# A zero column for the warm-up, K'V turned ahead of K'V, and a 304/208 split of the experts' second layer

## The chip, the core and the metric

The kernel runs on one core of a Trainium2 chip. The core has a matrix engine (TensorE: PE in the rows, with its weight loads as PEld), a vector engine (VectorE, DVE), an activation engine (ScalarE, ACT), GpSimd (POOL) and SyncE (SP), which here issues nearly all DMAs. Each engine runs its own instructions in order and waits on semaphores for the others. The metric is the device time of one execution in microseconds (us).

## The reference, cut to what matters

Three layers follow each other on 2304 tokens (4 batches of 576), all in float32.

```python
# 1. linear attention, 8 heads of 64; phi(x) = [exp(p - max|p|), exp(-(p - max|p|))], p = x @ w_phi (64 -> 128)
kv  = einsum('bhsf,bhsd->bhfd', phi(k), v);  z = phi(k).sum(s)
x   = (phi(q) @ kv) / (phi(q) @ z + 1e-6)                 # -> 2304 x 512
# 2. gated layer with RMS norm
xn  = x / rms(x) * g
x   = (silu(xn @ w_gate) * (xn @ w_val)) @ w_out          # 512 -> 1536 -> 512
# 3. soft mixture: 32 slots = 8 experts x 4
logits = x @ phi                                          # 2304 x 32
slot_input = softmax_over_tokens(logits).T @ x            # 32 x 512
slot_out[e] = relu(slot_input[e] @ w1[e]) @ w2[e]         # 512 -> 1024 -> 512, 8 experts
out = softmax_over_slots(logits) @ slot_out               # 2304 x 512
```

## The kernel before

The program has four stages, one after the other on PE.

**K stage** (0 to 116 us of the span). For each of 18 tiles of 128 tokens, K is projected (`P`, L501), DVE takes the largest magnitude and subtracts it (L505, L509), ACT takes both exponentials (`kp`, L522 and L523), and PE adds the products with V and with ones into three accumulators of the batch (`kacc`, L546 and L555). A batch has 576 tokens, so it ends in the middle of a tile: the loop then does `k.kv(parts[0])` for the old batch, `finish()`, `kn.project()` for the tile after next, and `k.kv(parts[-1])` for the new one. `finish()` makes an `Evac`: three copies of the accumulators to SBUF (`kvs0` to `kvs2`, L568 and L570), and three `turn`s, put into the list `fillers`. A turn is four PE transposes into a PSUM tile of three rotating ones (`misc`, shared with Q's projections `P` of L387) and two copies out of it into `kvt` (L592 on DVE for turn 1, L594 on ACT for turns 0 and 2). The loop pops one filler in each of a tile's two half steps, after `k.kv(parts[-1])`. Between these run the first block of Q (`Rows`: L387, L402, the products `o` of L447, the row scaling `y` of L467, the transposes `yT` of L474) and the conversion of nine weight pieces (`Conv`: L144, L146 on ACT; L154, L156, L122 on DVE, 1.2 us each). The order of instructions within this stage is made by a scheduler from the code, so a moved line moves others too.

At its start PE runs matmuls whose result nobody reads (`warm`, L608: `idle<-still`), four before the first projection and three after the second. `still` is a 128x256 tile that DVE sets to zero.

**Gated layer** (116 to 643 us): six blocks of 384 tokens, 12 strips of 128 hidden columns each. Its code is untouched.

**Router and slots** (643 to 653.6 us): `finish` in `post`; untouched.

**Experts and combination** (653.6 us to the end). 32 loads of 1 MB (`unit(n)`, L694) bring w1 (units 0 to 15) and w2 (16 to 31), in that order, into slots that come free as earlier weights are used. `fc1` multiplies the slot rows with w1 in 18 groups of four matmuls of 512 columns. `fc2(e, r, half)` does w2: `half` is which 512 of the 1024 hidden values, `r` which part of the 512 output columns (`RCOLS`: 256 and 256); a call is one group of four matmuls that run side by side on PE's four column strips. Before, unit 16 + e holds all hidden values of the first 256 columns and unit 24 + e those of the last 256. `slots(r)` copies the sum (DVE, L1118), adds the four strips by a matmul (`so`, L1120) and scales it (DVE, L1121, L1122). `combine(r, blk)` multiplies the weights of 384 tokens with it in nine matmuls (`op`, L1136), copies three tiles out (DVE and ACT in turn, L1140, L1142) and issues the output DMA of the block (L1146; L1144 one by one for block 0). The order of PE within the experts is the order of the code in `experts()` (it is `placed`).

Of the kernel before, what the change touches and what calls it, by code (L numbers as in the profile page):

```python
# [30 lines left out]
CFIRST = 7  # L31
WARM = 4
WARM2 = 3
RCOLS = [256, 256]
CEVERY = 3
PADDED = [3.5, 3.5, 3.5, 6, 6.5, 18.5, 13.5]
PLAST = [2, 2, 2, 6, 9, 15, 12]
# [29 lines left out]
def tile_kernel(ctx: ExitStack, tc: tile.TileContext, q2T, qT, kT, v, wbd, wg, wv, wo, rmsg, phi, w1, w2, consts, out):  # L67
# [409 lines left out]
    with ExitStack() as pk:  # L477
# [121 lines left out]
        ks = [K(sp, psk, kT, i, kb if i else dict(kb, P=("misc", 3))) for i in range(TILES)]  # L599
        ks[0].load(ACT)  # L600
        SP.dma_start(out=wbd_f, in_=wbd)
        still = sp.tile([128, 256], F32, tag="kvs0", name="still", bufs=1)
        DVE.memset(still, 0.0)
        DVE.memset(ones_sb, 1.0)
        idle = psk.tile([32, 256], F32, tag="acc0", name="idle", bufs=1)
        def warm(n, w):
            for _ in range(n):
                PE.matmul(out=idle[:, 0:w], lhsT=still[:, 0:32], rhs=still[:, 0:w], start=True, stop=True)  # L608

        warm(WARM, 256)  # L610
        for r in range(2):
# [23 lines left out]
        for i in range(TILES):  # L635
            k, kn = ks[i], ks[i + 2] if i + 2 < TILES else None
            if i + 4 < TILES:
                ks[i + 4].load()
            if i + 2 < TILES:
                ks[i + 2].load_v()  # L640
            parts = batch_parts(i)
            b = parts[0][0]
            ends = i * 128 + parts[0][2] == (b + 1) * SEQ

            def finish():
                ev = Evac(b)
                fillers.extend([lambda n=n: ev.turn(n) for n in range(3)])

            if len(parts) > 1:
                k.kv(parts[0])  # L650
                finish()
            if kn:
                kn.project()
                kn.shift(0)
                kn.shift(1)
            k.kv(parts[-1])
            for hf in range(2):
                if kn:
                    kn.exps(hf)
                n = 2 * i + hf - CFIRST  # L660
                if (n + 5) % 3 == 0 and 0 <= n + 5 and (n + 5) // 3 < NPRE:
                    placed(lambda: conv_load(sp, KCONV, sp), SP.engine)
                if n >= 0:
                    if n % 3:
                        conv_join()
                    else:
                        conv_parts()
                        conv_scale()
                if fillers:
                    fillers.pop(0)()  # L670
                for f in qsteps[2 * i + hf]:
                    f()
            if ends and len(parts) == 1:
                finish()
# [401 lines left out]
    with ExitStack() as p3:  # L1076
# [28 lines left out]
            ho.fill(lambda o, i: ACT.activation(out=o, in_=i, func=AF.Relu), h, 4 * half, 4 * half + 4)  # L1105

        def fc2(e, r, half):
            u = unit((2 + r) * NE + e).rearrange("p (k d) -> p k d", k=8)
            for c in range(4):
                k = 4 * half + c  # L1110
                PE.matmul(out=y2[r][32 * c:32 * c + 32], lhsT=ho[e, k], rhs=u[:, k],  # L1111
                          start=e == 0 and half == 0, stop=e == NE - 1 and half == 1)

        def slots(r):

# [32 lines left out]
        def experts():  # L1148
# [9 lines left out]
            turn1(1)  # L1158
            for e in range(2, NE):
                fc2(e, 0, 0)  # L1160
            for e in range(NE):
                fc2(e, 0, 1)
            blk = 0
            for e in range(NE):
                fc2(e, 1, 0)
                fc2(e, 1, 1)
                if e == 0:
                    slots(0)
                if e in (2, 5, 7):
                    for blk in range(blk, blk + (2 if e < 7 else 1)):  # L1170
                        combine(0, blk)
                    blk += 1
            slots(1)
            combine(0, blk)
# [7 lines left out]
def _layout(inputs):  # L1182
    import numpy as np

    def heads(a):
# [22 lines left out]
        "rmsg": np.asarray(inputs["moe_rms_g"]).reshape(4, 128).T,  # L1208
        "phi": np.asarray(inputs["moe2_phi"]).reshape(4, 128, NS).transpose(1, 0, 2).reshape(128, 4 * NS),
        "w1": np.asarray(inputs["moe2_w1"]).reshape(NE, 4, 128, 2, 512).transpose(0, 3, 2, 1, 4).reshape(NE, 2, 128, 2048),  # L1210
        "w2": np.asarray(inputs["moe2_w2"]).reshape(NE, 8, 128, 2, 256).transpose(0, 3, 2, 1, 4).reshape(NE, 2, 128, 2048),
        "consts": consts,
    }

# [19 lines left out]
```

## Time and profile before

| | us |
|---|---|
| median of 3 runs (700.24 to 700.74) | 700.58 |
| the profiled execution | 701.1 |
| its span | 699.3 |
| PE busy | 687.5 (98%) |
| DVE, ACT, POOL busy | 469.8, 328.1, 146.6 |
| end of PE's last instruction | 692.0 |

The profiled execution is 1.8 us longer than its span, and 0.5 us longer than the median. In the page's forty slices PE is at 90% or more in all but the first and the last, DVE at 80 to 90% or more in most of the first seven. The output DMAs fill the last 7 us alone.

### The profile page before, as it was taken

How to read it: one execution, taken by the hardware profiler on the slowest of the kernel's cores; microseconds unless marked ns; L12 is line 12 of the kernel's file. 1: busy time of each engine (PE TensorE's matmuls, PEld its weight loads, DVE VectorE, ACT ScalarE, POOL GpSimd, SP SyncE). 2: the span in 40 equal slices, each digit the busy share in tenths (PEclk: the TensorE clock that was granted, in tenths of full speed). 3: DMA queues.
4: the chain of work that ended last, by engine and by line, in shares of the span. 5: the costliest groups of instructions: out<-in, count | busy, mean ns of one | idle time of the engine just before them, and what ended most of it. 6: DMA issues, size and time to landing. Idle time of an engine off the chain costs nothing.

```text
span 699.3 us, 11901 instructions
## 1 busy us (share of the span) xinstructions
PE 687.5 (98%) x4715; PEld 570.8 (82%) x4715; DVE 469.8 (67%) x914; ACT 328.1 (47%) x686; POOL 146.6 (21%) x74
## 2 busy tenths in 40 slices
PE   8999999999999999999999999999999999999995
PEld 5667666988889898998979989899897999898453
DVE  4899995988875695766857669676685753323423
ACT  4878885687745444344432554425444231112202
POOL 0000000000003355133651336422364200000100
PEclk9999999999999999999999999999999999999997
DMA  7755534434210001010000100001000085477977
GB/s 258 256 186 175 193 123 166 144 121 164 78 40 27 7 23 32 0 58 12 24 0 1 57 13 24 0 1 57 1 1 0 1 314 228 180 264 276 372 303 260
DMA packets 24216, 77.66 MB, mean 111 GB/s; under 512 B 2528, under 2 KB 12640, under 8 KB 17760
## 3 DMA queue, kind: packets, MB, share of 16 engines
q1 hardware_dynamic: 24016, 76.64, 30.9%
q8 instruction: 37, 0.61, 0.4%
q10 hardware_dynamic: 144, 0.26, 0.1%
q14 instruction: 19, 0.16, 0.1%
HBM read 71.11 MB, written 5.78 MB: 110 GB/s over the span
## 4 chain that ended last, share of the span: by engine, by line
PE 96%; DMA 1%; ACT 1%; DVE 0%; issue 0%; SPq 0%; DVEq 0%; ACTq 0%
PE pv L952 22%; PE pg L952 22%; PE acc L977 7%; PE acc L978 7%; PE acc L979 7%; PE kacc L546 5%; PE num L221 4%; PE kacc L555 3%; PE P L501 3%; PE y L1111 2%; PE y L1095 2%; PE o L447 2%; PE P L387 1%; PE x2tp L742 1%; PE op L1136 1%; PE qP L313 1%
## 5 line engine op out<-in xcount | busy, mean ns | idle before, releaser
L952 PE MATMUL pv<-xnh,wv 128*128 128x384 f32 x576 | 117.1, 342 | 0.0
L952 PE MATMUL pg<-xnh,wg 128*128 128x384 f32 x576 | 114.7, 341 | 0.3 <-ACT xnh L119 0.3
L316 POOL PARTITION_ALL_REDUCE qe<-qe x32 | 51.9, 1634 | 295.7 <-ACT qe L315 286.5
L952 PEld LDWEIGHTS pg<-xnh,wg 128*128 128x128 f32 x576 | 102.8, 188 | 6.2 <-ACT xnh L119 0.7
L952 PEld LDWEIGHTS pv<-xnh,wv 128*128 128x128 f32 x576 | 101.9, 188 | 4.9 <-DVE qe L346 3.4
L347 POOL PARTITION_ALL_REDUCE qe<-qe x32 | 82.1, 2613 | 85.0 <-DVE qe L346 66.4
L119 ACT CAST hh<-t 128x384 fp32r<-128x384 f32 x72 | 36.6, 509 | 115.8 <-PE acc L978 75.5
L977 PE MATMUL acc<-wo,hh 128*128 128x512 f32 x216 | 87.1, 403 | 0.0
L978 PE MATMUL acc<-wo,hh 128*128 128x512 f32 x216 | 86.1, 398 | 0.0
L979 PE MATMUL acc<-wo,hl 128*128 128x512 f32 x216 | 85.2, 394 | 0.0
L122 DVE TENSOR_TENSOR hl<-t,hh 128x384 fp32r<-128x384 f32 x72 | 40.0, 556 | 65.1 <-ACT hh L119 64.9
L960 DVE SCALAR_TENSOR_TENSOR t<-t,pg 128x384 f32<-128x384 f32 x72 | 39.6, 550 | 57.7 <-ACT t L959 57.5
L959 ACT ACTIVATE t<-pg 128x384 f32<-128x384 f32 x72 | 35.1, 487 | 72.5 <-PE pg L952 72.1
L952 PE MATMUL pg<-xnl,wg 128*128 128x384 f32 x288 | 64.9, 341 | 0.0
L952 PE MATMUL pv<-xnl,wv 128*128 128x384 f32 x288 | 62.4, 338 | 0.0
L964 DVE TENSOR_TENSOR t<-t,pv 128x384 f32<-128x384 f32 x72 | 39.5, 549 | 25.3 <-PE pv L952 24.3
L952 PEld LDWEIGHTS pg<-xnl,wg 128*128 128x128 f32 x288 | 51.9, 188 | 1.5 <-DVE xnl L122 0.9
L952 PEld LDWEIGHTS pv<-xnl,wv 128*128 128x128 f32 x288 | 51.7, 188 | 0.0
L979 PEld LDWEIGHTS acc<-wo,hl 128*128 128x128 f32 x216 | 40.6, 188 | 10.2 <-DVE hl L122 0.3
L977 PEld LDWEIGHTS acc<-wo,hh 128*128 128x128 f32 x216 | 40.8, 189 | 7.4 <-issue 0.3
L978 PEld LDWEIGHTS acc<-wo,hh 128*128 128x128 f32 x216 | 40.6, 188 | 6.4
L546 PE MATMUL kacc<-kp,vt 128*64 128x256 f32 (+1 forms) x320 | 39.8, 386 | 0.0
(206 smaller groups left out, 1047.3 us busy)
## 6 DMA issues: line engine op xcount, KB each, us to landing
eu<-in_w_dram SPq DMA_DIRECT2D x32, 1024.0 KB, 6.4
wraw<-in_wg_dram SPq DMA_DIRECT2D x6, 1024.0 KB, 4.8
wraw<-in_wv_dram SPq DMA_DIRECT2D x6, 1024.0 KB, 5.7
wraw<-in_wo_dram SPq DMA_DIRECT2D x6, 1024.0 KB, 5.1
qraw<-in_qT_dram SPq DMA_DIRECT2D x32, 192.0 KB, 2.3
vt<-in_v_dram SPq DMA_DIRECT2D x18, 256.0 KB, 2.9
raw<-in_kT_dram SPq DMA_DIRECT2D x17, 256.0 KB, 3.2
out_dram<-ob SPq DMA_DIRECT2D x10, 384.0 KB, 3.5
```

The lines of the kernel that those rows point to most:

```text
L119: ACT.copy(out=hi, in_=src)
L122: (lo_eng or POOL).tensor_tensor(out=lo, in0=src, in1=hi.bitcast(F32), op=ALU.subtract)
L316: POOL.partition_all_reduce(e[:, 0], e[:, 1], channels=128, reduce_op=bass_isa.ReduceOp.absmax)
L347: POOL.partition_all_reduce(e[hh][:, 1], u, channels=128, reduce_op=bass_isa.ReduceOp.add)
L546: PE.matmul(out=kva[o0:o0 + 64, hh // 2], lhsT=self.vt[r0:r1, h], rhs=kp[r0:r1, hh].rearrange("p s f -> p (s f)"), start=first and hh < 2, ...
L952: PE.matmul(out=p, lhsT=w[:, a, c], rhs=x, start=n == 0, stop=n == 11)
L959: ACT.activation(out=t, in_=g, func=AF.Tanh, scale=0.5)
L960: DVE.scalar_tensor_tensor(out=t, in0=t, scalar=1.0, in1=g, op0=ALU.add, op1=ALU.mult)
L964: DVE.tensor_tensor(out=t, in0=t, in1=wide("v", m, xs), op=ALU.mult)
L977: PE.matmul(out=acc[i], lhsT=hh[:, s], rhs=w[:, 0], start=m == 0, stop=False)
L978: PE.matmul(out=acc[i], lhsT=hh[:, s], rhs=w[:, 1], start=False, stop=False)
L979: PE.matmul(out=acc[i], lhsT=hl[:, s], rhs=w[:, 0], start=False, stop=m == MF - 1)
```

## The change

- `still` becomes a constant column of zeros that GpSimd sets before the program starts; both operands of the unread products read it with a step of zero. DVE's memset goes.
- In the tile in which batch 1 begins (`b == 0` there), the first filler, turn 0 of batch 0's K'V, is popped before `k.kv(parts[-1])`; turns 1 and 2 each come one half step earlier.
- `RCOLS` becomes 304 and 208. w2 is laid out so that unit 16 + e holds the first 512 hidden values with all 512 columns and unit 24 + e the other 512. Each part r now reads all 16 units. The order in `experts()`: all of r = 0 for the first halves, the second halves of experts 0 to 5, two groups of r = 1 (expert 0), the second halves of experts 6 and 7, then the other 14 groups of r = 1 with `slots(0)` after two of them and one block of `combine(0, .)` after 5, 7, 10, 12 and 14.

```diff
-RCOLS = [256, 256]
+RCOLS = [304, 208]
...
-        still = sp.tile([128, 256], F32, tag="kvs0", name="still", bufs=1)
-        DVE.memset(still, 0.0)
+        still = nc.const_aps.tensor(0.0, [128, 1], F32)
...
-                PE.matmul(out=idle[:, 0:w], lhsT=still[:, 0:32], rhs=still[:, 0:w], start=True, stop=True)
+                PE.matmul(out=idle[:, 0:w], lhsT=still.to_broadcast([128, 32]), rhs=still.to_broadcast([128, w]), start=True, stop=True)
...
                 kn.shift(1)
+            if fillers and b == 0:
+                fillers.pop(0)()
             k.kv(parts[-1])
...
         def fc2(e, r, half):
-            u = unit((2 + r) * NE + e).rearrange("p (k d) -> p k d", k=8)
+            u = unit((2 + half) * NE + e).rearrange("p (k d) -> p k d", k=4)
...
-            for e in range(NE):
+            for e in range(6):
+                fc2(e, 0, 1)
+            second = [(e, half) for e in range(NE) for half in range(2)]
+            for e, half in second[:2]:
+                fc2(e, 1, half)
+            for e in range(6, NE):
                 fc2(e, 0, 1)
             blk = 0
-            for e in range(NE):
-                fc2(e, 1, 0)
-                fc2(e, 1, 1)
-                if e == 0:
+            for n, (e, half) in enumerate(second[2:]):
+                fc2(e, 1, half)
+                if n == 1:
                     slots(0)
-                if e in (2, 5, 7):
-                    for blk in range(blk, blk + (2 if e < 7 else 1)):
-                        combine(0, blk)
+                if n in (4, 6, 9, 11, 13):
+                    combine(0, blk)
                     blk += 1
```

**PE, K stage, where batch 0 ends (29 to 46 us).** `kacc` are products of K' with V or with ones (the numbers are those of batch 1), `kvt` the transposes of a turn. Before:

```order
L546 MATMUL kacc_438<-kp,vt 64x256 x4
L546 MATMUL kacc_439<-kp,vt 64x256 x4
L555 MATMUL kacc_440<-kp,small 32x256 x8
L583 MATMUL kvt<-cst,kvs_413 128x128 x4
L387 MATMUL P<-wbd_f,qraw 128x256
L583 MATMUL kvt<-cst,kvs_415 128x128 x4
L387 MATMUL P<-wbd_f,qraw 128x256
L501 MATMUL P<-wbd_f,raw 128x128 x8
L546 MATMUL kacc_438<-kp,vt 64x256 x4
L546 MATMUL kacc_439<-kp,vt 64x256 x4
L555 MATMUL kacc_440<-kp,small 32x256 x8
L583 MATMUL kvt<-cst,kvs_417 128x128 x4
```

Now:

```order
L583 MATMUL kvt<-cst,kvs_411 128x128 x4
L546 MATMUL kacc_443<-kp,vt 64x256 x4
L546 MATMUL kacc_444<-kp,vt 64x256 x4
L555 MATMUL kacc_445<-kp,small 32x256 x8
L583 MATMUL kvt<-cst,kvs_413 128x128 x4
L387 MATMUL P<-wbd_f,qraw 128x256
L583 MATMUL kvt<-cst,kvs_415 128x128 x4
L501 MATMUL P<-wbd_f,raw 128x128 x3
L387 MATMUL P<-wbd_f,qraw 128x256
L501 MATMUL P<-wbd_f,raw 128x128 x5
L546 MATMUL kacc_443<-kp,vt 64x256 x4
L546 MATMUL kacc_444<-kp,vt 64x256 x4
```

The first turn stands ahead of the sixteen products, the other two follow one place earlier each, and Q's second projection stands behind three of the next tile's eight K projections.

**DVE, end of the K stage (96 to 109 us).** From the scaling of the last product `o` of Q's block 0 towards the row scaling; `wt`, `wv`, `wo` are weight pieces. Before:

```order
L122 TENSOR_TENSOR wv_1310<-wt,wv_1310 128x1024
L154 SCALAR_TENSOR_TENSOR wt<-wt,wraw 128x1024
L450 TENSOR_SCALAR rd<-o 128x6
L592 COPY kvx<-kvt 128x2x2x64
L451 RECIPROCAL rd<-rd 128x6
L592 COPY kvx<-kvt 128x2x2x64
L452 TENSOR_TENSOR y<-o,rd 128x3x128
L505 TENSOR_REDUCE mx<-P 128x4 x2
L509 TENSOR_TENSOR pr<-P,mx 128x512 x2
L464 TENSOR_SCALAR ms<-ms 128x3
L156 SCALAR_TENSOR_TENSOR wt<-wraw,wt 128x1024
L196 TENSOR_SCALAR rs<-ms 128x3
```

Now:

```order
L450 TENSOR_SCALAR rd<-o 128x6
L156 SCALAR_TENSOR_TENSOR wt<-wraw,wt 128x1024
L451 RECIPROCAL rd<-rd 128x6
L592 COPY kvx<-kvt 128x2x2x64
L452 TENSOR_TENSOR y<-o,rd 128x3x128
L592 COPY kvx<-kvt 128x2x2x64
L505 TENSOR_REDUCE mx<-P 128x4 x2
L509 TENSOR_TENSOR pr<-P,mx 128x512 x2
L464 TENSOR_SCALAR ms<-ms 128x3
L122 TENSOR_TENSOR wv_1308<-wt,wv_1308 128x1024
L196 TENSOR_SCALAR rs<-ms 128x3
L122 TENSOR_TENSOR wo_1369<-wt,wo_1369 128x1024
```

Between `L450` and the row scaling (L467, further on in both) stood two operations of 128x1024 (`L156` and, later, `L122` of `wo`); now there are three, since `L122` of `wv` has come from in front of `L450`.

**PE, experts, around the end of the first column part.** `y` with the lower number is part 0, with the higher part 1; `eu` are the loads. Before:

```order
L1111 MATMUL y_6490<-eu_6390,ho 32x256 x4
L1111 MATMUL y_6491<-eu_6653,ho 32x256 x8
L1120 MATMUL so<-y2s,cst 96x256
L1111 MATMUL y_6491<-eu_6669,ho 32x256 x8
L1111 MATMUL y_6491<-eu_6679,ho 32x256 x8
L1136 MATMUL op<-SO_6494,cT 128x256 x18
L1111 MATMUL y_6491<-eu_6724,ho 32x256 x8
L1111 MATMUL y_6491<-eu_6734,ho 32x256 x8
L1111 MATMUL y_6491<-eu_6744,ho 32x256 x8
L1136 MATMUL op<-SO_6494,cT 128x256 x18
```

Now (`eu_6663` and `eu_6669` are units 30 and 31, the last two loads):

```order
L1111 MATMUL y_6488<-eu_6649,ho 32x304 x4
L1111 MATMUL y_6489<-eu_6289,ho 32x208 x4
L1111 MATMUL y_6489<-eu_6619,ho 32x208 x4
L1111 MATMUL y_6488<-eu_6663,ho 32x304 x4
L1111 MATMUL y_6488<-eu_6669,ho 32x304 x4
L1111 MATMUL y_6489<-eu_6291,ho 32x208 x4
L1111 MATMUL y_6489<-eu_6625,ho 32x208 x4
L1120 MATMUL so<-y2s,cst 96x304
L1111 MATMUL y_6489<-eu_6293,ho 32x208 x4
L1111 MATMUL y_6489<-eu_6631,ho 32x208 x4
L1111 MATMUL y_6489<-eu_6335,ho 32x208 x4
L1136 MATMUL op<-SO_6492,cT 128x304 x9
```

Part 0 is complete only after the last load; before, it needed none of the last eight. The blocks of `op` stand one at a time instead of two. SP's order of loads is the same.

## Rows read from the trace of the kernel before

**Rows 1.** The page, part 4: shares of the chain that ended last.

```profile
PE 96%; DMA 1%; ACT 1%; DVE 0%; issue 0%; SPq 0%; DVEq 0%; ACTq 0%
```

**Rows 2.** Timeline, all engines, first 12 us: start, length, engine, line, operation, count.

```profile
0.24 0.10 POOL L1223 MEMSET const-float32-0.0<- 128x1 f32 x1 [0.24 <-issue]
...
0.85 0.27 DVE L603 MEMSET still<- 128x256 f32 x1 [0.85 <-PEq L1223]
1.08 0.09 DVE L604 MEMSET small<- 128x32 f32 x1
...
1.18 3.62 PE L608 MATMUL idle<-still 128*32 128x256 f32 x8 [1.18 <-DVE small L604]
...
4.73 2.42 PEld L501 LDWEIGHTS P<-wbd_f,raw 64*128 64x128 f32 x32 [0.81 <-DMA raw<-in_kT_dram]
...
7.27 1.48 PE L608 MATMUL idle<-still 128*32 128x256 f32 x6
```

**Rows 3.** The chain that ended last, first 46 us: start, length, what.

```profile
36.68 1.06 ACT wraw L146
...
38.77 0.55 ACT kv L594 x2
...
41.16 1.88 PE kacc L546 x16
43.03 1.00 PE kacc L555 x16
44.03 0.59 PE kvt L583 x4
...
44.84 0.43 PE P L387 x2
```

**Rows 4.** Timeline, all engines, 29 to 46 us.

```profile
31.48 0.58 ACT L570 COPY kvs<-kacc 128x512 f32<-128x512 f32 x1
...
35.99 1.21 DVE L154 SCALAR_TENSOR_TENSOR wt<-wt,wraw 128x1024 uint32<-128x1024 uint32 x1
...
39.25 0.41 DVE L592 COPY kv<-kvt 128x256 f32<-128x256 f32 x1
...
39.36 0.70 PE L387 MATMUL P<-wbd_f,qraw 128*128 128x256 f32 x2 [1.47 <-ACT kv L594]
```

**Rows 5.** Timeline, all engines, 96 to 111 us.

```profile
97.98 0.16 DVE L450 TENSOR_SCALAR rd<-o 128x6 f32<-128x6 f32 x1 [0.32 <-PE o L447]
...
108.30 1.27 DVE L467 TENSOR_SCALAR y<-y,ms 128x512 f32<-128x512 f32 x3
...
109.72 0.96 PEld L474 LDWEIGHTS yT<-cst,y 128*128 128x128 f32 x9 [0.41 <-DVE y L467]
```

**Rows 6.** The chain that ended last, 640 us to the end.

```profile
668.27 0.86 PE y L1111 x16
669.13 0.60 PE hp L1102 x4
669.74 7.04 PE y L1111 x128
...
680.16 2.73 PE y L1111 x48
682.89 0.91 PE op L1136 x18
```

**Rows 7.** SP's last load (unit 31) alone: its issue, and the time to its landing.

```profile
L694 SPq DMA_DIRECT2D eu<-in_w_dram x1: 328/328/328, 663.2 to 663.2; - x1
...
DMA to landing us min/median/max: 15.6/15.6/15.6
```

**Rows 8.** SP's output DMA of block 5 of part 0 alone.

```profile
L1146 SPq DMA_DIRECT2D out_dram<-ob x1: 462/462/462, 688.7 to 688.7; - x1
```

**Rows 9.** Two stretches: engines' busy time and counts, clock, DMA share, GB/s.

```profile
660.00:676.00 16.00, 16.00 (x216) 7.18 (x212) 2.79 (x6) 1.39 (x5) 0.00 (x0) 1.00 1.01 420
694.00:696.00 2.00, 0.00 (x0) 0.00 (x0) 0.00 (x0) 0.00 (x0) 0.00 (x0) 0.50 1.03 345
```

More of the change, by code (lines that the diff above doesn't have):

```diff
@@ L1107, in fc2 @@
         def fc2(e, r, half):
-            u = unit((2 + r) * NE + e).rearrange("p (k d) -> p k d", k=8)
+            u = unit((2 + half) * NE + e).rearrange("p (k d) -> p k d", k=4)
             for c in range(4):
-                k = 4 * half + c
-                PE.matmul(out=y2[r][32 * c:32 * c + 32], lhsT=ho[e, k], rhs=u[:, k],
-                          start=e == 0 and half == 0, stop=e == NE - 1 and half == 1)
+                PE.matmul(out=y2[r][32 * c:32 * c + 32], lhsT=ho[e, 4 * half + c], rhs=u[:, c, cols[r]],
+                          start=e == half == 0, stop=e == NE - 1 and half == 1)
         def slots(r):
@@ L1210, in _layout @@
         "w1": np.asarray(inputs["moe2_w1"]).reshape(NE, 4, 128, 2, 512).transpose(0, 3, 2, 1, 4).reshape(NE, 2, 128, 2048),
-        "w2": np.asarray(inputs["moe2_w2"]).reshape(NE, 8, 128, 2, 256).transpose(0, 3, 2, 1, 4).reshape(NE, 2, 128, 2048),
+        "w2": np.asarray(inputs["moe2_w2"]).reshape(NE, 2, 4, 128, 512).transpose(0, 1, 3, 2, 4).reshape(NE, 2, 128, 2048),
         "consts": consts,
```

## The prediction, made before the changed kernel ran

> **What bounds the kernel now.** I read the page's chain first: the work that ended last is PE's for 96% of the span [rows 1], so from the first projection to 692 us a microsecond counts if PE gets it, and other engines matter where PE waits for them. The largest wait inside the span is 1.47 us in the K stage, on ACT's copy of a K'V turn [rows 4]; it lies in the stretch that the second part of the change moves. PE also stands still for the first 1.18 us, until DVE has set `small` [rows 2]. Behind PE's end there are 7 us in which nothing runs but output DMAs, at 345 GB/s with the DMA engines full [rows 9]. So three places decide: the start, the end of batch 0, and the experts with the output behind them. Everything between hangs on PE and shifts as a whole, loads included, since their issues wait for PE to free their slots. Times below are in the clock of the profiled execution (701.1 us, span 699.3); the differences are applied to the median, 700.58, because the 0.5 us between the two is not in any stage that changes.
>
> **Start: -0.3 us.** DVE sets `still` for 0.27 us, then `small`, and PE's first product begins as `small` ends, at 1.18 [rows 2]. The zero column is written by GpSimd at 0.24 [rows 2] and is there for the program anyway, so the new first product waits for no DVE work. It can begin when the engines are let go, by DVE's row at about 0.85: 0.33 earlier. The eight passes take 3.62 us, and PE takes up the projection at 4.73, behind them [rows 2]; its last operand came in the row's own wait, 0.81 us that PEld lays to the K tile's DMA, so it was there by about 4.3 and the projection can follow at 4.4. What could eat the gain is the clock: these passes take 0.45 us each, the six behind the projection 0.25 [rows 2], so the clock rose between them. If it rises at the same moment as before, the projection runs more of its passes at the half rate and about half the gain is lost; if it rises with PE's earlier start, nothing is lost, and one that rises while the first four products run gives up to half of 1.2 us more. Range 0.15 to 0.9; I take 0.3, near PE's own shift. Reading the operand with a step of zero costs nothing here: the count of passes is the same.
>
> **End of batch 0: -1.4 us.** Before, PE does sixteen products, a turn, Q's projection and a turn, then waits 1.47 us at Q's next projection [rows 4], because its PSUM tile is the one that the first turn filled and ACT's copies of it stand behind `wraw` (to 37.74) and two exponentials, to 39.32 [rows 3]. The change puts the first turn ahead of the sixteen products. Its input is written by 32.06 [rows 4], and PE arrives about 33.6, so it doesn't wait. Then PE: turn 0.59 to 34.2, products 1.88 and 1.00 to 37.1, turn 0.59 to 37.7, half of a 0.43 to 37.9, turn 0.59 to 38.5 (prices from rows 3), three of eight K projections 0.4 to 38.9. The projection that waited now needs the tile of the second turn, whose copies are DVE's. DVE has, from 36.0, two conversions of 1.21 and two copies of 0.41 [rows 4], less a little overlap: 39.0. So about 0.1 of the 1.47 stays. ACT's copies of the first turn move ahead of four exponentials (0.55 us for the pair); those exponentials serve products two tiles later, so PE doesn't see it. No DMA moves. Bounds: 0.3 if one more 1.2 us operation comes in front of DVE's copies, 1.5 if nothing waits. I take 1.4.
>
> **End of the K stage: +0.7 us.** The scheduler has also moved DVE's conversions. Before, PE's transposes `yT` started at 109.72, and the weight load's wait was for DVE's row scaling (108.30 + 1.27 = 109.57) [rows 5]: no slack. DVE's last wait for PE was at 97.98, for `o` [rows 5]; from there it had two conversions of 1.2 us on the way, now three. PE's own work from `o` to `yT` is the same. So if PE comes 1.7 us earlier to `o`, DVE still waits for it there, and then needs up to 1.2 us more, of which the 0.3 to 0.45 in which it used to wait on PE behind `o` absorb a part: PE waits 0.7. Bounds 0 (DVE makes it up elsewhere) and 1.0.
>
> **Experts and output: +1.5 us.** One group of 256 columns takes 7.04/16 = 0.44 us [rows 6]; by columns 304 take 0.52 and 208 take 0.36, and the sum over 32 groups is unchanged.
> 1. Part 0 ended at 669.74 + 14 x 0.44 = 675.9 [rows 6]. Now: 668.27 + 2 x 0.52 + 0.60 + 12 x 0.52 + 2 x 0.36 = 676.8, expert 6 to 677.4. Expert 7 needs unit 31, which lands at 663.2 + 15.6 = 678.8 [rows 7]: PE waits 1.4, and part 0 ends at 679.3, 3.4 later.
> 2. The rest of part 1 is 14 x 0.36 = 5.0 instead of 7.04: -2.0. `so` over 304 columns: +0.1.
> 3. Two blocks of `op` took 0.91, and six groups behind them 2.73 instead of 6 x 0.44 = 2.64 [rows 6], so about 0.1 a change. Four blocks now stand singly and are a fifth wider: 4 x 0.08 + 0.2 for two more bursts, and the first matmuls of a burst are slower than its mean: 0.5 to 0.9, I take 0.8.
> 4. Block 5 of part 0, issued at 688.7 [rows 8], comes 3.4 - 2.0 + 0.1 + 0.8 = 2.3 later, 691.0; DVE's order around it is as before.
> 5. From there the DMA engines are full to the end. Rows of 1 KB went at 345 GB/s and rows of 8 KB at 420 [rows 9]: on 16 engines 47.5 and 312 ns a row, so about 9.7 ns and 0.037 ns a byte; 832 bytes 40.4, 1216 bytes 54.6 (estimates). Block 5: 384 x 54.6/16 = 1.3 instead of 1.15. Part 1: 2304 x 40.4/16 = 5.8 instead of 6.85. Together -0.9.
> Sum +1.4 to +1.5. Bounds: 0 if the load doesn't hold PE, +2.5 if narrow rows take as long as the old ones. The load's wait is the largest term and the firmest: eight loads before the end come at 420 GB/s, one in 2.5 us, and no term above brings the last one forward relative to PE.
>
> Part 1's rows now begin 1216 bytes into a row of the output; no row of this trace shows such a start. The Trainium skill, "DMA: Bandwidth & Descriptors", section "How a descriptor splits into AXI transactions", says that transfers are cut at 256-byte boundaries and that a start off a boundary pays for the bytes before it. 1216 is 4 x 256 + 192, so by the page 832 bytes would cost four pieces, as 1024 did, and the sum would be 1.0 us more.
>
> **Sum.** -0.3 - 1.4 + 0.7 + 1.5 = +0.5: 701.1. A measurement of this kernel can tell about 0.2% from no change, 1.4 us: 699.2 and 702.0 are the marks.
>
> **Rivals.**
> 1. *The spread output pays* (faster). If PE isn't held at expert 7, because the last load lands some 1.4 us earlier relative to PE than the trace shows, the experts cost nothing and the total is -1.0: 699.6; with DVE in time at the end of the K stage, 698.9. For it: landings in a row of queued loads differ. Against: it needs 1.4 of 15.6 us, at 420 GB/s of a full queue. Chance 0.17, half below the mark.
> 2. *Narrow rows are no cheaper* (slower). The output drain of part 1 keeps its 6.85 us, since a row costs its start and not its bytes: total +1.5, 702.1. It decides from 1 us on, that is if an 832-byte row takes 47 ns. For it: 8 times the bytes gave only 6.6 times the time; against: that leaves 9.7 ns of fixed cost, not 47. Chance 0.16, half above the mark.
> 3. *The wait at the end of batch 0 changes its name* (the change doesn't do what it says). PE waits as long for DVE's copies of the second turn as it did for ACT's: -0.3 there instead of -1.4, total +1.6, 702.2. DVE has 3 us of work in front of the copies, and one more operation suffices. Chance 0.11, nearly all above.
> 4. *The clock rises earlier at the start*: -0.6 more, 700.5, no change. Chance 0.06.
>
> The forecast keeps 0.50, with its own range 700.0 to 702.0. Faster: 0.08 from rival 1, 0.04 from the forecast's lower terms falling together: 0.12. Slower: 0.08 + 0.09 + 0.03: 0.20. The rest, 0.68, can't be told from no change. Eight in ten lie between 699.0 (rival 1 in full) and 702.9 (rivals 2 or 3 with the forecast's larger bounds).
>
> **What would show it.** The first unread product at 0.8 to 0.9 us. No wait over 0.3 us of PE between 33 and 42 us; a wait for DVE's copies there speaks for rival 3. A new wait of PE at `yT`, for L467. A wait of 1 to 1.6 us of PE on the DMA of `eu` in `fc2`, before the last group of 304 columns; none speaks for rival 1. Output at or under 335 GB/s behind PE's end, in a stretch of about 5.8 us for part 1; 280 GB/s speaks for rival 2. The prediction is wrong if PE gains over 2 us before 640 us, or if the output ends earlier than now relative to the first `fc1`.

## The result, and the profile after

The changed kernel takes 706.25 us (median of 4 runs, 705.45 to 706.77) where the kernel before, on the same chip, takes 700.66 (median of 4): ratio 1.0071, 95% interval 1.0055 to 1.0086. It is slower, by 5.0 us by the ratio and 5.6 by the medians. The forecast was 701.1 in a range of 699.0 to 702.9, no difference that can be told; it was wrong, and the range did not hold the time. The profiled execution after takes 706.6 us with a span of 704.8; before it was 701.1 and 699.3.

The two traces, laid side by side by PE's instructions (starts from the timeline of PE, issues and landings from SP's and the DMAs' rows):

| stretch | before | after | difference | forecast |
|---|---|---|---|---|
| start to the first `kacc` | 9.60 | 9.18 | -0.42 | -0.3 |
| to the first `o` (end of batch 0) | 39.80 | 40.41 | +0.61 | -1.4 |
| to the fourth `o` | 45.76 | 47.94 | +2.18 | 0 |
| to the first `pg` (end of the K stage) | 21.40 | 21.83 | +0.43 | +0.7 |
| to the first `fc1` | 537.04 | 536.87 | -0.17 | 0 |
| to the first `so` (two groups behind part 0's end) | 23.11 | 26.92 | +3.81 | +3.4 |
| to the issue of block 5 | 11.99 | 11.04 | -0.95 | -1.1 |
| to the last landing | 9.63 | 9.62 | 0 | -0.9 |

PE is at 90% or more in all of the forty slices but the last two. Of the 5.5 us that the span grew, 3.9 are busy time (687.5 to 691.4 us, with the same 4715 instructions) and 1.6 idle time. So most of the loss is no idle time, and a list of waits doesn't show it.

**Start.** Timeline of PE, after; columns are start, length, engine, line, operation, shapes, count, and in brackets the wait and what ended it. It answers to [rows 2].

```profile
0.77 3.59 PE L607 MATMUL idle<-const-float32-0.0 128*32 128x256 f32 x8 [0.77 <-PEq L1226]
4.33 2.58 PE L501 MATMUL P<-wbd_f,raw 64*128 64x128 f32 x32
```

The first product waits for no DVE work any more, and the projection follows 0.41 us earlier than before.

**End of batch 0.** Timeline of PE, then of ACT, after. These answer to [rows 4].

```profile
33.07 0.66 PE L583 MATMUL kvt<-cst,kvs 128*128 128x128 f32 x4
33.65 1.94 PE L546 MATMUL kacc<-kp,vt 64*64 64x256 f32 x16
...
37.45 0.60 PE L583 MATMUL kvt<-cst,kvs 128*128 128x128 f32 x4
37.98 0.71 PE L501 MATMUL P<-wbd_f,raw 64*128 64x128 f32 x6
40.23 0.70 PE L387 MATMUL P<-wbd_f,qraw 128*128 128x256 f32 x2 [1.54 <-ACT kv L594]
40.86 0.93 PE L501 MATMUL P<-wbd_f,raw 64*128 64x128 f32 x10
41.72 1.95 PE L546 MATMUL kacc<-kp,vt 128*64 128x256 f32 x16
```

```profile
36.29 0.69 ACT L594 COPY kv<-kvt 128x256 f32<-128x256 f32 x2
...
38.38 0.68 ACT L523 ACTIVATE kp<-pr 128x512 f32<-128x512 f32 x1
38.90 1.15 ACT L146 ACTIVATE wraw<-wraw 128x1024 uint32<-128x1024 uint32 x1
39.89 0.28 ACT L594 COPY kv<-kvt 128x8 f32<-128x8 f32 x2
```

The first turn went ahead as planned and its copies too (36.29). The wait is still there, 1.54 us for 1.47. It now ends with ACT's small copies (128x8, two of them, 39.89) of the third turn: by that wait, Q's second projection has got the PSUM tile of that turn, and those copies stand behind four exponentials and `wraw`. The rest of the +0.61 is PE's own work. Of the next tile's K projection six instructions stand ahead of Q's projection and ten behind it, and they take 0.71 and 0.86 us where the sixteen together take 1.09: +0.48. Without the wait it is 38.32 us from the first `kacc` to the first `o` in each of the seven profiles with the K stage of before, and 38.87 in each of the four with that of the change.

**Where PE is busy for longer.** Timeline of PE around 84 us, before and then after.

```profile
83.49 1.16 PE L501 MATMUL P<-wbd_f,raw 64*128 64x128 f32 x16
84.58 1.95 PE L546 MATMUL kacc<-kp,vt 128*64 128x256 f32 x16
86.46 1.07 PE L555 MATMUL kacc<-kp,small 128*32 128x256 f32 x16
```

```profile
84.22 1.16 PE L501 MATMUL P<-wbd_f,raw 64*128 64x128 f32 x8
85.30 0.65 PE L546 MATMUL kacc<-kp,vt 128*64 128x256 f32 x2
85.88 1.16 PE L501 MATMUL P<-wbd_f,raw 64*128 64x128 f32 x8
86.96 1.94 PE L546 MATMUL kacc<-kp,vt 128*64 128x256 f32 x14
88.83 1.07 PE L555 MATMUL kacc<-kp,small 128*32 128x256 f32 x16
```

A projection of K is eight products on 64 rows, four for the upper and four for the lower half of the array, written in turn; in the trace each product is two instructions, so sixteen. Before, all sixteen take 1.09 us (83.49 to 84.58). After, eight come first, by their time those of one half, one `kacc` product (two instructions) behind them, and the other eight last: each eight takes 1.08 us alone, and all of it 2.74. The fourteen `kacc` instructions that are left take 1.87 us where sixteen took 1.88. From the start of the projection to L555 it is 4.61 us for 2.97, which is the 1.64 us that are lost from the third to the fourth `o`. At 65 us, a `kacc` product has been pulled ahead of a projection in the same way:

```profile
65.34 0.65 PE L546 MATMUL kacc<-kp,vt 128*64 128x256 f32 x2
65.91 1.17 PE L501 MATMUL P<-wbd_f,raw 64*128 64x128 f32 x16
67.01 1.94 PE L546 MATMUL kacc<-kp,vt 128*64 128x256 f32 x14
```

It takes 0.57 us alone and the other fourteen instructions 1.87 (to 68.88), which makes the 0.54 us that are lost from the second to the third `o`.

**End of the K stage.** Timeline of DVE, and of PE with its weight loads, after; they answer to [rows 5].

```profile
111.41 1.28 DVE L467 TENSOR_SCALAR y<-y,ms 128x512 f32<-128x512 f32 x3
```

```profile
112.20 2.09 PE L474 MATMUL yT<-cst,y 128*128 128x128 f32 x12
112.74 0.75 PEld L474 LDWEIGHTS yT<-cst,y 128*128 128x128 f32 x7 [0.26 <-DVE y L467]
114.22 1.95 PE L546 MATMUL kacc<-kp,vt 128*64 128x256 f32 x16
```

DVE's row scaling ends at 112.69, behind the start of the transposes, and their weight loads wait for it. No wait of PE itself is listed, but the twelve transposes take 2.02 us to the next product where they took 1.69 (109.73 to 111.42): +0.33 of the +0.43.

**Experts.** Timeline of PE, and the window of the drain of part 1 (length; busy time and count of five engines; clock; DMA share; GB/s), after; they answer to [rows 6, 9].

```profile
681.80 1.42 PE L1111 MATMUL y<-eu,ho 128*32 128x304 f32 x24 [1.80 <-DMA eu<-in_w_dram]
683.15 0.75 PE L1120 MATMUL so<-y2s,cst 128*96 128x304 f32 x2
683.83 1.26 PE L1111 MATMUL y<-eu,ho 128*32 128x208 f32 x24
685.02 0.69 PE L1136 MATMUL op<-SO,cT 32*128 32x304 f32 x9
685.64 0.91 PE L1111 MATMUL y<-eu,ho 128*32 128x208 f32 x16
...
691.84 0.59 PE L1120 MATMUL so<-y2s,cst 128*96 128x208 f32 x2
```

```profile
698.00:701.00 3.00, 0.00 (x0) 0.00 (x0) 0.00 (x0) 0.00 (x0) 0.00 (x0) 0.56 1.03 321
```

PE waits 1.80 us for the last load, as forecast in kind. (The stretch from the first `fc1` holds 16 groups of `fc1`, two an expert, not 18.) The chain from there to the issue of block 5 is shorter, as forecast, but the drain behind block 5 gives nothing back.

### The profile page after: what moved, and what is told of

Same layout as the page of the kernel before. It is cut to its first block, busy times and chain, and to the rows that moved or that the text cites. A ratio compares the mean times of both kernels' runs of the same rounds, so it can differ in the third digit from the quotient of the medians.

```text
span 704.8 us, 11895 instructions
## 1 busy us (share of the span) xinstructions
PE 691.4 (98%) x4715; PEld 572.1 (81%) x4715; DVE 469.8 (67%) x913; ACT 328.0 (47%) x686; POOL 146.7 (21%) x74
## 4 chain that ended last, share of the span: by engine, by line
PE 92%; DMA 3%; DVE 2%; ACT 1%; issue 0%; SPq 0%; DVEq 0%; ACTq 0%
PE pg L953 22%; PE pv L953 22%; PE acc L978 7%; PE acc L979 7%; PE acc L980 7%; PE kacc L546 4%; PE num L221 4%; PE P L501 2%; DMA eu<-in_w_dram 2%; PE kacc L555 2%; PE o L447 2%; PE P L387 1%; PE y L1096 1%; DMA wraw<-in_wo_dram 1%; PE op L1136 1%; PE x2tp L743 1%
## 5 line engine op out<-in xcount | busy, mean ns | idle before, releaser
L122 DVE TENSOR_TENSOR hl<-t,hh 128x384 fp32r<-128x384 f32 x72 | 40.1, 556 | 65.0 <-ACT hh L119 64.9
L546 PE MATMUL kacc<-kp,vt 128*64 128x256 f32 (+1 forms) x320 | 41.1, 386 | 0.0
```

Of the source, the lines that this page charges most:

```text
L122: (lo_eng or POOL).tensor_tensor(out=lo, in0=src, in1=hi.bitcast(F32), op=ALU.subtract)
L546: PE.matmul(out=kva[o0:o0 + 64, hh // 2], lhsT=self.vt[r0:r1, h], rhs=kp[r0:r1, hh].rearrange("p s f -> p (s f)"), start=first and hh < 2, ...
```

## The experiments

Thirteen kernels ran. Each ratio is to the kernel before on the same chip, with its 95% interval. Expectations give times for a kernel before of 700.6 us or so; it took 700.32 to 700.87 on the chips of these runs. Where a stretch of the trace is given, it begins with the first `kacc`, so that the chance of the clock's rise (last section) is not in it. The wait at the end of batch 0 still differs from profile to profile: with the K stage of before it was 1.15 to 1.47 us, and to the first `pg` it took 106.64 to 106.96.

**The three parts alone.** `zero_only`, `turn_only` and `experts_only` are the kernel before with one part of the diff each.

> The kernel before with the zero column alone. Theory: the traces of before and after show the first product 0.41 us earlier, the projection 0.41 us earlier and the clock's rise 0.45 us earlier, and the order of the instructions behind the start is that of before. So the whole program moves by 0.4 us: 700.2 to 700.3 where before is 700.6, ratio 0.9994. Rival: the 0.4 us are absorbed at the wait of 1.47 us at the end of batch 0, which hangs on ACT and not on PE: ratio 1.0000, and that wait is 1.9 us.

> The kernel before with the early turn alone. Theory (split pairs): the changed kernel lost 2.8 us in the K stage against before, of it 0.6 between 32 and 46 us and 2.0 between 65 and 89 us, where products that stood in pairs on two halves of the array now stand alone, and 0.4 at the yT transposes. All of this comes from this part, and the 0.4 us of the zero column are missing: 700.6 + 3.1 = 703.7, ratio 1.0045, first pg product 3.0 to 3.2 us later than before. Rival (a later start of the loads or another part is to blame): first pg within 1 us of before's 116.6, about 701.5.

> The kernel before with the third part alone (experts' second layer and output). Theory: the same terms as in the changed kernel: PE waits 1.8 us for the last of the sixteen loads of the second layer ahead of the last group of 304 columns, part 0 ends 3.8 us later, block 5 is issued 2.9 us later, and behind that nothing is given back although 832-byte rows are cheaper, so 700.6 + 2.9 = 703.5, ratio 1.0041. Rival (the wait is longer only because the K stage shifted the loads against each other): the wait is 1.4 us or less and the total 702.1 or less.

Measured: 699.77, 0.9993 (0.9984 to 1.0002); 703.52, 1.0043 (1.0029 to 1.0056); 702.82, 1.0040 (1.0025 to 1.0055). The three effects add up to 1.0076, the change gave 1.0071: as far as intervals of this width can tell, the parts don't act on each other. Of the early turn's +3.0 us the trace shows all between the first `kacc` and the first `pg`: 110.05 us for 106.96. In `experts_only` the wait for the last load was 1.28 us, the rival's size, and from the first `fc1` to the last landing it takes 46.90 us for 44.73: a time between the two theories. The wait differs from profile to profile (last section).

```profile
677.66 1.42 PE L1110 MATMUL y<-eu,ho 128*32 128x304 f32 x24 [1.28 <-DMA eu<-in_w_dram]
```

The zero column can't be told from no change; its rival, a wait of 1.9 us at the end of batch 0, is not there (1.34).

**Are the split pairs the loss?** `tied12` is the changed kernel with the projection and the `kacc` products around 84 us chained in the order in which they are written; `pairs2` does the same at 65 us too. "Products" are single instructions in some of the expectations.

```diff
+            def step():
                 if kn:
                     kn.project()
...
                 k.kv(parts[-1])
+            if i in [12]:             # pairs2: [9, 12]
+                tied(step, PE.engine)  # each PE instruction behind the one written before it
+            else:
+                step()
```

> The changed kernel with one edit: at one of the two places where the scheduler pulled the eight products of a projection apart (around 84 us), the projection's and the next kacc products are chained in the order in which they are written, so that upper-half and lower-half products alternate again. The early turn stays. Theory (split pairs): two half-projections that take 1.1 us each go back to 1.1 for both, and two kacc products find their partners: 1.1 to 1.45 us less, 704.8 to 705.2 where the changed kernel has 706.25. Rival (PE waits for DVE to free the second half's tile, and the split only fills that wait): the order goes back, a wait of about 1 us of PE appears ahead of the projection, and the time stays at 706.0 or more.

> The changed kernel with the products chained in the written order at both places (around 65 and 84 us). At 65 us the projection then waits for DVE if its tile isn't free, and the scheduler puts a K'V turn in that wait. Theory (lost partners): from the second o product to the third it takes 18.0 to 18.2 us where the changed kernel has 18.45 and before 17.91, and 21.2 to 21.4 from the third to the fourth as in tied12: 705.0 to 705.4. Rival (the wait for DVE is as long as what the split costs): 18.4 or more from the second to the third.

`tied12`: 705.23, 1.0074 (1.0052 to 1.0096). `pairs2`: 704.66, 1.0058 (1.0044 to 1.0071). Such intervals don't separate them from the change (1.0071). The stretches do, at 84 us. From the third to the fourth `o` it takes 21.28 us in both (before 20.30, change 21.94). So 0.66 of 1.64 come back, and the rest, 0.98, has another cause, which now shows as a wait. PE in `tied12` (L512 and L557 are L501 and L546 of the others):

```profile
84.01 0.49 PE L512 MATMUL P<-wbd_f,raw 64*128 64x128 f32 x2
85.03 1.13 PE L512 MATMUL P<-wbd_f,raw 64*128 64x128 f32 x14 [0.54 <-DVE pr L520]
86.09 1.95 PE L557 MATMUL kacc<-kp,vt 128*64 128x256 f32 x16
```

DVE, whose conversions have moved too, is late with the subtraction that frees the second half's tile: the first product (84.01) stands alone, then PE waits 0.54 us, and the projection takes 2.08 us for 1.09. Both theories hold in part: the split cost more than the wait that it filled. At 65 us `pairs2` gained nothing, as its rival says (18.43 us from the second to the third `o`, change 18.45, before 17.91): there the scheduler put a K'V turn between the first product and the other fourteen instructions, so one product still stands alone. This run doesn't tell the causes apart at that place. What does, though with another order on DVE, are the runs `turn_dve` and `late_wo` below: the early turn without a split at 65 and 84 us, 17.91 and 20.30 us, as before.

**What a product without a partner costs.** `halves` is the kernel before with two loops exchanged in `project`:

```diff
-                for c in range(4):
-                    for hf in range(2):
+                for hf in range(2):
+                    for c in range(4):
```

> The kernel before with one edit: each projection of K writes its eight products for the upper 64 rows first and the eight for the lower 64 behind them, where before the two halves alternate. The same products with the same operands. Theory (products on different halves of the array run side by side, and one that stands alone takes as long as two): each of the eighteen projections takes 2.0 to 2.2 us instead of 1.16, together 15 to 18 us more, less what waits for DVE absorb: 710 to 719. Rival (the pull of the two halves apart costs only what stands between them): 702 or less.

714.22, 1.019 (1.0172 to 1.0209). PE in `halves`, first behind the wait at the end of batch 0, then in a later tile (before: the row at 83.49 above):

```profile
43.01 1.07 PE L387 MATMUL P<-wbd_f,qraw 128*128 128x256 f32 x2 [2.26 <-ACT kv L594]
44.01 3.09 PE L501 MATMUL P<-wbd_f,raw 64*128 64x128 f32 x16
47.04 3.41 PE L546 MATMUL kacc<-kp,vt 128*64 128x256 f32 x16
...
68.66 1.71 PE L501 MATMUL P<-wbd_f,raw 64*128 64x128 f32 x16
70.29 1.95 PE L546 MATMUL kacc<-kp,vt 128*64 128x256 f32 x16
```

From its first product to the next other one a projection takes 1.64 us for 1.09: +0.55, times sixteen 8.8 us. The theory said 2.0 to 2.2, which is the price when other products stand between the halves. The rest of the 13.4 us is a longer wait at the end of batch 0 (2.26 for 1.47) and the clock: the record has it at 1.2 GHz from 43.21 to 50.04 us, behind that wait, where it costs about 3.4 us (an estimate, half of that time). So the total lies in the theory's range partly by luck: 4.2 of the 13.4 us are not its mechanism. The Trainium skill, "TensorE: Matmul & The Clock Gate", section "The mechanism" of its part on packing, says that a weight load overlaps products in flight only where the row group differs. The two times fit that, 1.09 us in turn and 1.64 half by half; the overlap itself no row shows.

**Is the wait at the end of batch 0 ACT's third turn?** `turn_dve`: the kernel before with the zero column and the early turn, and

```diff
-                    if n == 1:
+                    if n == 1 or (n == 2 and self.b == 0):
                         DVE.tensor_copy(o, i)
...
+            if i == 17:
+                placed(step, PE.engine)   # the last tile's kacc behind yT
```

> The kernel before with the zero column and the early turn, and with two edits: the copies of the last turn of batch 0 are DVE's instead of ACT's, and the last tile's kacc products are chained behind the yT transposes so that they stay together. No product that has a partner on the other half of the array loses it behind batch 0. Theory (the wait of 1.54 us is for ACT's copy of the last turn, which shares its PSUM bank with the tile that Q's second projection writes): DVE has its copies done by about 39.2, so the wait is 0.3 to 0.8 us, and the first pg product is 0.4 + 0.7 to 1.2 us earlier than before: 699.0 to 699.5, ratio 0.998. Rival (the wait goes to another holder of the bank or to another engine, as it did in the change): a wait of 1.2 us or more stays between 37 and 42 us, and only the zero column's 0.4 us are left: 700.0 or more.

701.13, 1.0008 (0.9999 to 1.0017): the rival's time, but not by its wait. The wait for ACT's copies is gone altogether (from 37 to 42 us PE doesn't stand still). PE and DVE there:

```profile
37.72 0.93 PE L501 MATMUL P<-wbd_f,raw 64*128 64x128 f32 x10
38.60 0.69 PE L387 MATMUL P<-wbd_f,qraw 128*128 128x256 f32 x2
39.21 0.71 PE L501 MATMUL P<-wbd_f,raw 64*128 64x128 f32 x6
39.85 1.95 PE L546 MATMUL kacc<-kp,vt 128*64 128x256 f32 x16
...
43.75 1.49 PE L501 MATMUL P<-wbd_f,raw 64*128 64x128 f32 x16
```

```profile
37.70 0.75 DVE L592 COPY kv<-kvt 128x256 f32<-128x256 f32 x2
...
38.70 0.17 DVE L592 COPY kv<-kvt 128x8 f32<-128x8 f32 x1
```

Q's second projection starts at 38.60, ahead of DVE's copies of the third turn (38.70), so here it has another tile than that turn's; the theory's shared bank is not what this run shows, and which tile it has is not on record. And not all of the wait is gained: from the first `kacc` to the first `o` it takes 39.12 us for 39.80. The projection around Q's takes 0.88 and 0.64 us for 1.09, and the next one 1.42 (43.75 to 45.17): +0.76 of PE's own work. To the first `pg` it takes 107.72 for 106.96. What was gained is waited for, and more, at the transposes:

```profile
109.23 1.34 PE L474 MATMUL yT<-cst,y 128*128 128x128 f32 x9 [0.69 <-DVE y L467]
111.02 0.55 PE L474 MATMUL yT<-cst,y 128*128 128x128 f32 x3 [0.45 <-ACT xraw L475]
```

The 0.69 is the wait that the forecast named; the 0.45 stands at my own chain and is not in `late_wo`, which lacks it.

**Does DVE hold the end of the K stage?** `late_wo` drops that chain and puts DVE's conversion of the last `wo` piece behind the row scaling; `late2_d3` puts the last `wv` piece there too, and gives DVE the last batch's third turn, so that ACT's conversion of `xn` doesn't stand behind it.

```diff
+            self.scaled = nc.cur_bb.bb.instructions[-1].name      # the last L467
...
                         conv_parts()
+                        # DVE instructions of this call, n == 27 (late2_d3: 24 and 27):
+                        tc.add_manual_dep(ins, q0.scaled, nosync, reason="placed")
...
-                    if n == 1 or (n == 2 and self.b == 0):
+                    if n == 1 or (n == 2 and self.b in (0, NB - 1)):     # late2_d3
```

> The kernel before with the zero column, the early turn, the copies of batch 0's last turn on DVE, and one more edit: DVE's conversion of the last w_out piece of the K stage stands behind its row scaling ahead of the yT transposes instead of ahead of it. The chain of the run before this one (turn_dve) is dropped: the order of PE is without split pairs by itself. Theory (DVE sets the end of the K stage: in the run turn_dve PE gained 0.7 us at the end of batch 0 and waited 0.69 us for that row scaling): with 1.1 us less ahead of it DVE is in time, the wait at yT is under 0.2, and from the first kacc product to the first pg product it takes 106.1 to 106.4 us where before has 107.0: 699.2 to 699.8 where before is 700.7, ratio 0.998 to 0.9985. Rival (something else at the end of the K stage, ACT's copies of yT or the conversion of xn, holds the first pg product): 106.8 or more.

> The run late_wo with two more edits at the end of the K stage: DVE's conversion of the last w_val piece stands behind the row scaling too, and the small copies of the last batch's last turn are DVE's, so that ACT's conversion of xn no longer stands behind them. Theory (in late_wo 0.33 us were lost between the yT transposes and pg because DVE's scaling was still late, and 0.30 because ACT's xn conversion waits behind a copy that waits for PE): from the first kacc to the first pg product 106.0 to 106.3 us where late_wo has 106.7 and before 107.0: ratio 0.9980 to 0.9986. Rival (the chain from the scaling to pg has another link of the same length): 106.6 or more.

`late_wo`: 700.11, 0.9989 (0.9981 to 0.9998); first `kacc` to first `pg` 106.71 us, nearer to the rival and within what the K stage of before shows: the transposes (from 108.83) still took 2.09 us for 1.77, and DVE's scaling ended at 109.32. `late2_d3`: 699.14, 0.9979 (0.9970 to 0.9988); 105.93 us, a little under the theory. PE there:

```profile
109.08 1.77 PE L475 MATMUL yT<-cst,y 128*128 128x128 f32 x12
...
115.46 1.44 PE L958 MATMUL pg<-xnh,wg 128*128 128x384 f32 x6 [0.27 <-ACT xnh L119]
```

No wait at the transposes, and 1.0 us gained in the K stage: 0.7 to the first `o`, 0.4 from the last `o` to the first `pg` (21.05 us for 21.41). No run has the later conversions without the early turn, so whether they would gain without it is open. This version is faster than both kernels, by 1.5 us than before and, by the two ratios, by some 6.5 than the change.

**The experts.** `cover` is the third part alone with six groups of part 1, not two, ahead of expert 7, and one block each after 4, 5, 7, 8 and 10 of the ten groups that are left. `experts_256` is the third part alone with `RCOLS = [256, 256]`. `spread_old` is the kernel before, old layout and columns, with single blocks; `spread_old2` the same with the last block behind the last group.

```diff
-            for e in range(6):
+            for e in range(NE - 1):
                 fc2(e, 0, 1)
-            for e, half in second[:2]:
+            for e, half in second[:6]:
                 fc2(e, 1, half)
-            for e in range(6, NE):
-                fc2(e, 0, 1)
+            fc2(NE - 1, 0, 1)
```

```diff
-                if e in (2, 5, 7):
-                    for blk in range(blk, blk + (2 if e < 7 else 1)):
-                        combine(0, blk)
+                if n in (4, 6, 9, 11, 13):      # spread_old2: 4, 7, 10, 13, 15 of 0 to 15
+                    combine(0, blk)
```

> The third part alone, as in the run of it, with one edit: expert 6's group of 304 columns stands where the others stand, and six groups of 208 columns instead of two stand ahead of expert 7's group; the last five blocks of part 0 are closer together. Theory (the wait for the last load is lost time that work can cover): four groups more at 0.36 us take 1.4 of the 1.3 to 1.8 us of PE's wait, PE ends 1.3 us earlier relative to the first layer's start, and the output with it: 701.5 where the third part alone has 702.8. Rival (the output's own queue sets the end from part 0's first block on): part 0 ends no earlier, its first output row leaves at the same time, and 4.7 MB from there at some 325 GB/s end within 0.5 us of where they end now: 702.4 or more.

> The third part alone with 256 and 256 columns: new layout of the second layer, new order, old width. Theory: PE comes to expert 7 1.0 us earlier and waits so much longer (2.3 us) for the last load; part 0 ends about as before, fourteen groups of part 1 cost 0.44 instead of 0.36 us (1.1 more), five op blocks 0.04 less each, and the drain of part 1 0.5 more: 703.5 to 704.5 where the third part alone has 702.8. Rival (the narrow second part buys nothing): 702.8 or less.

> The kernel before with its old columns (256 and 256) and its old layout of the second layer; only the last blocks of part 0 stand singly between groups of 256 columns, as in the change. Theory: single blocks cost PE about 0.25 us for a pair that is split, 0.5 us in all, and the last block of part 0 is issued no later than before because it no longer waits for expert 7: 700.3 to 700.9, no difference from before. Rival (spreading itself is what delays the output in the change): over 701.5.

> As spread_old (old columns, old layout), with the last single block behind the last group, where before has it, so that it covers DVE's copy ahead of the second so product again. Theory: 0.64 us of the 1.5 us that spread_old cost were PE's wait for that copy, the rest is what four single blocks cost PE against two pairs (0.7 us): 701.3 to 701.7, ratio 1.0010 to 1.0015. Rival (single blocks delay the output by more than PE's own time, because each one's copies and its issue stand in a row): 702 or more.

`cover`: 702.39, 1.0024 (1.0015 to 1.0033); the interval holds the theory's time and the rival's. PE doesn't wait for the load any more, and `so` of part 1 starts 33.72 us behind the first `fc1` (35.09 without cover), but the last landing comes only 0.94 earlier (45.96 for 46.90; before 44.73). So both theories hold in part: PE gained 1.4, of which 0.9 reached the end of the output; part 0 still ends with the last load (its `so` 26.32 us behind `fc1` for 26.40). `experts_256`: 705.14, 1.0062 (1.0041 to 1.0082), above the theory's 704.5; 1.92 us of wait for the forecast 2.3, and 47.49 us from `fc1` to the last landing. The narrow second part is worth 0.6 us in the traces and 1.5 by the two ratios, whose intervals overlap: that it gains is likely, its size is not shown. `spread_old`: 702.37, 1.0025 (1.0016 to 1.0034); the rival's time, but of its 1.5 us 0.64 are a fault of my edit, which left DVE's copy ahead of `so` without a block to cover it:

```profile
687.39 0.64 PE L1120 MATMUL so<-y2s,cst 128*96 128x256 f32 x2 [0.64 <-DVE y2s L1118]
```

`spread_old2`: 700.99, 1.0004 (0.9994 to 1.0013), whose interval holds most of the theory's ratios and no change, but not the rival's 702; in the trace `so` of part 1 comes 33.36 us behind `fc1` for 32.70, so four single blocks cost PE 0.66 us, and the last landing 0.62.

## Why the prediction was wrong, point by point

- **Start, -0.3.** The first product came at 0.77, as forecast. What followed hangs on when the clock rises, which differs from run to run by more than this term (last section). With the clock's rise at 4.96 (`turn_dve`) and 4.98 (`turn_only`) the first `kacc` came at 8.92 and 9.15: 0.2 us at equal rise, near the half that the text named for a rise that doesn't follow PE. On the mean of seven profiles each nothing shows, so the mechanism is borne out and the size is not; that the table has -0.42 is luck.
- **End of batch 0, -1.4.** Wrong in the step "The projection that waited now needs the tile of the second turn, whose copies are DVE's". DVE had those copies done at 38.71 (37.96 and 0.75), as forecast, but the wait ended with ACT's copies of the third turn at 40.2. I took the rotation of the tiles for the order of their allocation, without looking at which tile the program really gives. The third rival was the right one in kind (the wait changes its name, at about its old length), with ACT's third turn in place of DVE's second. A second step failed here too: "three of eight K projections 0.4" prices a part of a projection by its share. The two parts took 1.57 us for 1.09, and `turn_dve`, without the wait, kept 0.7 of its 1.47 us.
- **From the first `o` to the fourth, 0.** This is the largest error, 2.2 us. The step that failed is "Everything between hangs on PE and shifts as a whole": PE's own work between the three places was put at no change. (That it is the same "from `o` to `yT`" was said of the last `o`, and held to 0.1 us.) The instructions are the same; their order is not, and the rows show that the order is the price: the two broken-up places make the 0.54 and the 1.64 us. The changed order had the pattern in plain sight at the end of batch 0, where eight projections in a row became three, Q's, and five. I compared counts and looked for waits. Of the loss at 84 us 0.66 us are shown to be the split (`tied12`); without the split the other 0.98 would be DVE's lateness, 0.54 of it a wait. What made the order change at 65 us was not separated.
- **End of the K stage, +0.7.** Right in mechanism: `turn_dve`, where PE does come early, waits 0.69 us there for the row scaling. In the change, where PE came 2.4 us late (97.53 for 95.16), DVE still cost 0.33, as slower transposes. So the early turn could not have paid by itself with DVE's conversions in this order.
- **Experts, +1.5.** The load's wait was forecast as 1.4; the four profiled executions with the change's order of the experts had 1.80, 1.28, 0.98 and 1.10. Part 0's end at +3.4 and the shorter rest at -1.1 were right within 0.4. The drain's -0.9 was not. The price of a row was right: groups of 128 rows of 832 bytes began 0.343 us apart in `experts_only`, of 1024 bytes 0.386 us before, 0.73 us less to the last group. The ends were not priced: block 5's wide rows took 0.1 more, the last 128 rows 0.81 to 1.00 us where they took 0.56 to 0.66, and the landing behind the last row 0.55 for 0.34. The sum is -0.17 in `experts_only` and 0 in the profile after.
- **Rivals.** Narrow rows that cost as much as wide ones: refuted, 42.0 ns a packet of 832 bytes for 48.6 of 1024, and 321 GB/s where that rival needed 280. The Trainium skill, "DMA: Bandwidth & Descriptors", section "How a descriptor splits into AXI transactions", gives these rows, which start off a 256-byte boundary, four pieces like the old ones; the packets here don't show that. A spread output that pays: no, in the change's order the load held PE by 0.98 us or more, and `cover`, where it doesn't, is slower than before too.

The range failed for the same reason as the sum: the rivals were waits, the rows of the output and the clock at the start, and none allowed PE to be slower at the same work.

## What to carry to other kernels

Where products run side by side on parts of the array, the order of the instructions is a cost by itself: after any edit that a scheduler may answer, compare the runs of each product in the order, not only their counts, and price a run that is broken up. Ask of a wait that you mean to remove which buffer the waiting instruction gets afterwards, and who is late next; here it took three edits at DVE and ACT until a gain reached the end of the stage. In this kernel the layout that lets the first part of the output finish on half of the second layer's loads was worth more than a shorter last part.

## What the runs showed of the hardware

- Sixteen 64-row instructions take 1.09 us when the halves alternate, 1.64 half by half, and 2.16 as two eights with other products between them. The single records of the traces account for it: a run's first start is followed by the next one after 0.21 us, then they come every 0.11 us, two instructions at a time where the halves alternate and one where they don't, and 0.20 us behind the last start a product of another kind begins. That is 8 starts, 13 (in `halves` three of each half still pair up in the middle), and twice 8.
- The clock's rise at the start came between 3.92 and 6.57 us in the profiled executions of kernels that start alike, and the first `kacc` with it between 8.67 and 9.73. Seven with the zero column (first product at 0.77) and seven without it (1.18, `halves` left out) have the same mean, 9.23 and 9.22. One pair of profiles can't show a gain at the start.
- In `halves` a wait of 2.26 us at the end of batch 0 was followed by 6.83 us at 1.2 GHz, in which a projection took 3.02 us for 1.64; waits of 1.5 to 1.9 us in the other kernels were not.
- The last of 32 loads landed 24.6 to 25.4 us behind the first `fc1`, though it was issued 9.57 us behind it each time; the four kernels with the change's order of the experts span the whole 0.8 us, so that much of a wait for a load is chance.
